# Where late expert weights stand in the DMA queue of an attention-plus-experts kernel

## The chip, the cores and the metric

The kernel runs on one core of a Trainium2 chip. The metric is the device time of one execution in microseconds. Before the change it is 280.02 us (median of 3 runs, 279.81 to 280.1). The profiled execution has a span of 281.0 us. Five engines appear: TensorE (PE, with its weight loads as PEld), VectorE (DVE), ScalarE (ACT), GpSimd (POOL) and SyncE (SP). Data comes and goes through 16 DMA engines.

## What is computed

Windowed attention with a few global positions is followed by a mixture of experts in which each token goes to exactly one expert and each expert takes exactly `cap` tokens, in the order of the gate's scores.

```python
# attention: B, H, S, D = 4, 8, 768, 64; 8 global positions, window of 96
keep = is_global | is_local
scores = np.where(keep, scale * q @ k.T + bias, -1e9)      # bias: slope of the head x distance
x = softmax(scores) @ v                                    # -> (N, D) = (3072, 512)

# experts: E, F = 8, 1024; cap = N // E = 384
for idx in np.argsort(-(x @ w_gate).flatten()):            # greedy, balanced
    tok, e = idx // E, idx % E
    if assigned[tok] < 0 and counts[e] < cap: assigned[tok] = e; counts[e] += 1
for e in range(E):
    mask = assigned == e
    out[mask] = np.maximum(x[mask] @ w1[e], 0.0) @ w2[e]
```

## The kernel before

The kernel has three stages. In the first (to about 145 us) attention is computed, and its result, cast to bf16, is written to a DRAM tensor `x_tok` by DMAs of SyncE. In the second (to about 183 us) the assignment is found by a few rounds on PE and DVE; between these rounds TensorE computes "early work": 128 tokens for each of the experts 0 to 3, whose assignment is certain before the rounds are done. In the third the other tokens go through the eight experts. Each expert has three slabs of 128 tokens; for experts 0 to 3 (`EX = 4`) one slab was early work and two are left.

All weights are fp32 in DRAM and are cast to bf16 by the DMA that loads them. Those of experts 0 and 1 (`W_EARLY = 2`) and 2 come during attention. Those of 3 to 7 are the "late weights": two loads for each expert, in this order, taken from a list one at a time.

```python
def late_tiles(pool, es):
    for e in es:
        w_late[e] = (pool.tile([128, NKC, F_DIM], BF16, ...), pool.tile([128, NFC, DM], BF16, ...))
        lates.append((w_late[e][0], moe_w1[e]...))
        lates.append((w_late[e][1], moe_w2[e]...))
...
late_tiles(w2pool, range(3, N_EXP - 2))          # experts 3, 4, 5
gp = ...tile_pool(name="gp", bufs=9, ...)        # gathered rows, xe
fp = ...tile_pool(name="fp", bufs=2, ...)        # their transposes, xT
hp = ...tile_pool(name="hp", bufs=2, ...)        # hidden layer, hT
op = ...tile_pool(name="op", bufs=4, ...)        # output rows, ot

def late_weights(pin=True):
    if lates:
        dst, s_ = lates.pop(0)
        ins = nc.gpsimd.dma_start(dst, s_)
        if pin:
            tc.keep_in_program_order(ins)

for _ in range(6):                               # at the end of attention
    late_weights(False)
```

Weight loads, gathers of token rows and scatters of output rows are all issued by GpSimd. A gather reads 128 rows of `x_tok` by an index tile; a scatter writes 128 rows of `out` by one.

```python
def gather(e, slabs, pin=True):
    for t in slabs:
        s = TSLAB * e + t
        xe = gp.tile([128, DM], BF16, tag="xe", name=f"xe_{s}")
        ins = nc.gpsimd.indirect_dma_start(out=xe, ..., in_=x_tok[:, :],
                  in_offset=bass.IndirectOffsetOnAxis(ap=idi[:, s : s + 1], axis=0))
        ...
def scatter(ot, ids):
    s = nc.gpsimd.indirect_dma_start(out=out[:, :], out_offset=..., in_=ot, in_offset=None)
    ...
# second stage, when the assignment is known:
dispatch()                                       # writes the index tile idi
for e in range(EX):
    gather(e, range(1, TSLAB), False)            # two slabs for each of experts 0 to 3
```

The tiles of experts 6 and 7 lie in space that attention used, and are made known when the second stage has ended. Then comes the loop of the experts:

```python
late_tiles(w3pool, range(N_EXP - 2, N_EXP))      # experts 6, 7
...
load_x(0)                                        # PE transposes xe, DVE copies to xT
for e in range(N_EXP):
    xT_e = xT_of.pop(e)
    ns = len(slabs(e))
    if first:
        late_weights()
    if e + 2 < N_EXP and not (first and e + 2 < EX):
        gather(e + 2, slabs(e + 2))
    if first:
        late_weights()
    hT = hp.tile([128, NFC, CAP], BF16, tag="hT")
    for fc in range(NFC):                        # first layer: ph, then hT on ACT
        ...
    if e + 1 < N_EXP:
        load_x(e + 1)
    for j, t in enumerate(slabs(e)):             # second layer: po, then ot on DVE
        ...
        scatter(ot, idi[:, TSLAB * e + t : TSLAB * e + t + 1])
```

So in the kernel before the loads of experts 3, 4 and 5 are issued at the end of attention, those of expert 6 in the first round of this loop, those of expert 7 in the second, and the rows of expert 4 in the third.

Of the kernel before, what the change touches and what calls it, by code (L numbers as in the profile page):

```python
# [21 lines left out]
N_EXP = 8  # L22
# [18 lines left out]
EX = 4  # L41
# [4 lines left out]
def kernel(  # L46
# [850 lines left out]
# [4 lines that stand above are left out]
            if pin:  # L901
                tc.keep_in_program_order(ins)

    for _ in range(6):
        late_weights(False)

    def w1_of(e):
# [11 lines left out]
# [4 lines that stand above are left out]
            ins = nc.gpsimd.indirect_dma_start(  # L923
                out=xe, out_offset=None, in_=x_tok[:, :],
# [3 lines that stand above are left out]
            xes[s] = xe  # L928
# [64 lines left out]
    def routing(general):  # L993
      with ExitStack() as dctx:
# [11 lines left out]
        def tok_end():  # L1006
            if held:
                tok_out(*held.pop(0))
# [7 lines left out]
        def bc_e(t):  # L1016
            return t.rearrange("p (c o) -> p c o", o=1).to_broadcast([128, NCHUNK, N_EXP])
# [7 lines left out]
        def work(us):  # L1025
            while us > 0.0 and not general:
                if items:
                    cost, go = items.pop(0)
                    go()
                else:  # L1030
                    cost = 0.22
                    pw = ps_d.tile([128, 512], FP32, tag="po", name="pw")
                    nc.tensor.matmul(pw, lhsT=ident_bf, rhs=w1_early[:, 0, 0, 0:512], start=True, stop=True)
                us -= cost
# [6 lines left out]
        def best(X, Dg):  # L1041
            if X is None:
                UB = Lb
            else:
                nc.tensor.matmul(X, lhsT=negones, rhs=bc_c(Dg), start=False, stop=True)
                UB = Ub
                tok_begin()
                nc.vector.scalar_tensor_tensor(out=Ub[:, 8:32, :].rearrange("p c e -> p (c e)"), in0=X, scalar=0.0,
                                               in1=L_sb.rearrange("p c e -> p (c e)"),
                                               op0=ALU.is_gt, op1=ALU.add)  # L1050
            nc.vector.tensor_reduce(out=mn, in_=UB[:, 8:32, :], axis=AX.X, op=ALU.min)
            return UB
# [230 lines left out]
        if True:  # L1283
            work(0.7)
            X, Dg = None, None
            for kk in ROUND_KS:
                X, Dg = fast_round(kk, X, Dg)
            best(X, Dg)
            work(1.1)
            mnf = rpool.tile([128, NCHUNK], FP32, tag="mnf", name="mnf")  # L1290
            nc.vector.tensor_tensor(out=mnf, in0=mn, in1=cflag, op=ALU.subtract)
            nc.vector.tensor_tensor(out=M, in0=Ub[:, 8:32, :], in1=bc_e(mnf), op=ALU.is_le)
            dispatch()
            for e in range(EX):
                gather(e, range(1, TSLAB), False)
            vt = rpool.tile([128, EC, EX], BF16, tag="vt", name="vt")
            for lo_, hi_, at in ((16, 32, 0), (8, 10, 16)):
                n_ = hi_ - lo_
                nc.vector.tensor_tensor(
                    out=vt[:, at : at + n_, :], in0=Ub[:, lo_:hi_, 0:EX], op=ALU.is_gt,  # L1300
                    in1=mn[:, lo_ - 8 : hi_ - 8].rearrange("p (c o) -> p c o", o=1).to_broadcast([128, n_, EX]))
            nc.vector.tensor_tensor(out=vt, in0=vt, in1=Ck, op=ALU.mult)
            work(1.0)
            pf = ps_d.tile([128, 512], FP32, tag="pk", name="pf")
            nc.tensor.matmul(pf[0:1, 0:CE], lhsT=ones_bf[:, 0:1], rhs=Mf, start=True, stop=True, skip_group_check=True)
            nc.tensor.matmul(pf[0:1, CE : CE + EX * EC], lhsT=ones_bf[:, 0:1], rhs=vt.rearrange("p c e -> p (c e)"),
                             start=True, stop=True, skip_group_check=True)
            fc8 = dap.tile([1, N_EXP + 1], FP32)
            nc.vector.tensor_reduce(out=fc8[:, 0:N_EXP], in_=pf[0:1, 0:CE].rearrange("p (c e) -> p e c", e=N_EXP),
                                    axis=AX.X, op=ALU.add)  # L1310
            nc.vector.tensor_tensor(out=fc8[:, 0:N_EXP], in0=fc8[:, 0:N_EXP], in1=capv, op=ALU.subtract)
            nc.vector.tensor_tensor(out=fc8[:, 0:N_EXP], in0=fc8[:, 0:N_EXP], in1=fc8[:, 0:N_EXP], op=ALU.mult)
            nc.vector.tensor_reduce(out=fc8[:, N_EXP : N_EXP + 1], in_=pf[0:1, CE : CE + EX * EC], axis=AX.X, op=ALU.add)
            fm = dap.tile([1, 1], FP32)
            nc.vector.tensor_reduce(out=fm, in_=fc8, axis=AX.X, op=ALU.max)
            nc.vector.tensor_single_scalar(out=fi, in_=fm, scalar=0.0, op=ALU.is_gt)
            while items:
                work(0.1)
            while deferred:
                tok_begin()  # L1320
                tok_end()

    def experts(first):
        with ExitStack() as fctx:
            ps_t = fctx.enter_context(tc.tile_pool(name="ps_t", bufs=2, space=bass.MemoryType.PSUM))
            ps_h = fctx.enter_context(tc.tile_pool(name="ps_h", bufs=3, space=bass.MemoryType.PSUM))
            ps_o = fctx.enter_context(tc.tile_pool(name="ps_o", bufs=3, space=bass.MemoryType.PSUM))
            xT_of = {}

            def slabs(e):  # L1330
                return range(1 if first and e < EX else 0, TSLAB)

            def load_x(e):
                xT_e = fp.tile([128, NKC, TSLAB, 128], BF16, tag="xT_e", name=f"xT_{e}")
                for j, t in enumerate(slabs(e)):
                    xe = xes.pop(TSLAB * e + t)
                    pxe = ps_t.tile([128, NKC, 128], BF16, tag="pxe")
                    for kc in range(NKC):
                        nc.tensor.transpose(pxe[:, kc, :], xe[:, 128 * kc : 128 * kc + 128], ident_bf)  # L1339
                    nc.vector.tensor_copy(out=xT_e[:, :, j, :], in_=pxe)  # L1340
                xT_of[e] = xT_e

            if not first:
                gather(0, slabs(0))
            load_x(0)
            if not first:
                gather(1, slabs(1))
            for e in range(N_EXP):
                xT_e = xT_of.pop(e)
                ns = len(slabs(e))  # L1350
                if first:
                    late_weights()
                if e + 2 < N_EXP and not (first and e + 2 < EX):
                    gather(e + 2, slabs(e + 2))
                if first:
                    late_weights()
                hT = hp.tile([128, NFC, CAP], BF16, tag="hT")
                for fc in range(NFC):
                    ph = ps_h.tile([128, CAP], FP32, tag="ph")
                    for kc in range(NKC):  # L1360
                        nc.tensor.matmul(ph[:, 0 : 128 * ns], lhsT=w1_of(e)[:, kc, 128 * fc : 128 * fc + 128],  # L1361
                                         rhs=xT_e[:, kc, 0:ns, :].rearrange("p t n -> p (t n)"),
                                         start=(kc == 0), stop=(kc == NKC - 1))
                    nc.scalar.activation(hT[:, fc, 0 : 128 * ns], ph[:, 0 : 128 * ns], AF.Relu)  # L1364
                if e + 1 < N_EXP:
                    load_x(e + 1)
                for j, t in enumerate(slabs(e)):
                    po = ps_o.tile([128, DM], FP32, tag="po")
                    for fc in range(NFC):
                        nc.tensor.matmul(po, lhsT=hT[:, fc, 128 * j : 128 * j + 128],  # L1370
                                         rhs=w2_of(e)[:, fc, :], start=(fc == 0), stop=(fc == NFC - 1))
                    ot = op.tile([128, DM], FP32, tag="ot")
                    nc.vector.tensor_copy(out=ot, in_=po)  # L1373
                    scatter(ot, idi[:, TSLAB * e + t : TSLAB * e + t + 1])
# [53 lines left out]
```

The softmax here doesn't subtract the row's maximum and nothing guards it: scores larger than these inputs give would overflow.

## Time and profile before

| | before |
|---|---|
| time | 280.02 us (279.81 to 280.1) |
| span of the profiled execution | 281.0 us |
| PE busy | 249.5 us, 89% |
| DVE, ACT, POOL busy | 164.0, 142.1, 87.2 us |
| queue 0 (GpSimd's DMAs) | 26.22 MB |
| queue 1 (SyncE's DMAs) | 22.50 MB |
| late weights, as they land | 10 loads of 1024 KB |
| stretch from the first matmul of expert 0 to the last of expert 7 | 186.61 to 271.9 us |

The profile names an operation by its line, its engine and its tiles: `xe<-x_tok,idi` is a gather, `out_dram<-ot,idi` a scatter, `w<-in_moe_w_dram` a late weight load, `pxe<-ident_bf,xe` a transpose of gathered rows, `ph<-xT,w` a matmul of the first layer and `po<-w,hT` one of the second. In a timeline each line has the start and the length in microseconds, and in brackets how long the engine was idle before it and what ended that. A line on POOL for a DMA is the time in which GpSimd issues it, not the transfer.

### The profile page before, as it was taken

What the parts mean: (1) busy time and instruction counts of PE and PEld (TensorE: products, weight loads), DVE (VectorE), ACT (ScalarE), POOL (GpSimd) and SP (SyncE); (2) the same over time, 40 slices, a digit from 0 to 9 for tenths busy, and PEclk for the clock granted to TensorE, in tenths of its full rate; (3) what the DMA queues carried; (4) which work ended last, traced back from release to release, by engine and by line L of the source; (5) the groups of instructions that cost most, each with busy time, mean ns of one, the idle gap of its engine ahead of it and who ended that gap; (6) DMA issues with size and microseconds to landing.
All of it is one profiled execution on the core that took longest, in us unless ns stands there. A gap on an engine that the chain in (4) does not pass through costs nothing. (4 is left out here: it accounts for less than half of the span.)

```text
span 281.0 us, 7775 instructions
## 1 busy us (share of the span) xinstructions
PE 249.5 (89%) x3299; PEld 180.1 (64%) x3299; DVE 164.0 (58%) x346; ACT 142.1 (51%) x240; POOL 87.2 (31%) x145
## 2 busy tenths in 40 slices
PE   7799899999999999999988799867997499999960
PEld 2667687888888888868756666544775255655520
DVE  3978998988879796889257778311222113232120
ACT  5998879595977959534132213222444032523500
POOL 5040000110805720410480001376563444641240
PEclk9999999999999999999999999979999689999995
DMA  7993989499795999499979999735999622320221
GB/s 272 329 251 67 256 183 279 68 235 217 205 268 117 268 179 187 85 189 217 201 138 197 196 216 212 181 106 142 190 243 211 253 85 79 130 93 37 114 79 42
DMA packets 52570, 49.29 MB, mean 175 GB/s; under 512 B 29745, under 2 KB 44081, under 8 KB 52529
## 3 DMA queue, kind: packets, MB, share of 16 engines
q0 software_dynamic: 15680, 26.22, 44.7%
q1 hardware_dynamic: 36848, 22.50, 31.9%
q8 instruction: 28, 0.46, 0.7%
q14 instruction: 14, 0.11, 0.1%
HBM read 56.05 MB, written 9.44 MB: 233 GB/s over the span
## 5 line engine op out<-in xcount | busy, mean ns | idle before, releaser
L1364 ACT ACTIVATE hT<-ph 128x256 bf16<-128x256 f32 (+1 forms) x64 | 27.9, 438 | 55.6 <-PE ph L1361 46.6
L400 ACT ACTIVATE P<-ps 128x860 f32<-128x860 f32 (+1 forms) x46 | 39.4, 896 | 23.2 <-PE ps L382 22.4
L382 PE MATMUL ps<-qT,kA 32*128 32x215 f32 (+2 forms) x864 | 43.4, 333 | 2.5 <-ACT qT L347 2.5
L435 PE MATMUL po<-P,v 128*64 128x215 f32 (+6 forms) x576 | 42.9, 294 | 1.4 <-issue 1.0
L382 PEld LDWEIGHTS ps<-qT,kA 32*128 32x128 f32 x864 | 37.0, 185 | 7.4 <-issue 3.1
L435 PEld LDWEIGHTS po<-P,v 128*64 128x64 f32 x576 | 34.2, 136 | 10.8 <-issue 5.3
L415 DVE TENSOR_TENSOR P<-P,Wm 128x860 f32<-128x860 f32 (+1 forms) x32 | 32.9, 1044 | 6.6 <-ACT P L400 3.9
L1340 DVE COPY xT<-pxe 128x512 bf16<-128x512 bf16 x20 | 8.1, 423 | 46.6 <-PE pxe L1339 38.6
L931 POOL DMA_INDIRECT out_dram<-ot,idi x20 | 19.8, 991 | 37.8 <-DVE ot L1373 36.1
L1373 DVE COPY ot<-po 128x512 f32<-128x512 f32 x20 | 13.8, 692 | 24.8 <-PE po L1370 24.8
L322 DVE STREAM_TRANSPOSE RT<-RT 128x768 f32<-128x768 f32 x28 | 26.2, 959 | 3.5 <-DMA RT<-in_k_dram 3.4
L1370 PE MATMUL po<-w,hT 128*128 128x512 bf16 x112 | 27.7, 401 | 0.0
L466 PE MATMUL pr<-P,onesx 128*32 128x192 f32 (+11 forms) x768 | 27.6, 259 | 0.0
L1370 PEld LDWEIGHTS <-hT 128*128 128x128 bf16 x160 | 15.6, 101 | 18.5 <-issue 2.2
L466 PEld LDWEIGHTS pr<-P,onesx 128*32 128x32 f32 x768 | 24.7, 109 | 2.3 <-issue 0.3
L1361 PE MATMUL ph<-xT,w 128*128 128x384 bf16 (+1 forms) x160 | 25.1, 315 | 0.0
L332 ACT COPY kA<-RT 128x720 f32<-128x720 f32 (+2 forms) x18 | 24.4, 1354 | 0.1
L923 POOL DMA_INDIRECT xe<-x_tok,idi x20 | 19.3, 964 | 14.0 <-issue 4.7
L440 ACT COPY oT<-po 128x384 f32<-128x384 f32 x32 | 14.8, 493 | 13.7 <-PE po L435 7.3
L1361 PEld LDWEIGHTS <-w 128*128 128x128 bf16 x160 | 15.7, 98 | 9.3
L408 DVE TENSOR_TENSOR P<-P,Wm 128x860 f32<-128x860 f32 x16 | 16.5, 1060 | 7.1 <-ACT P L400 7.1
L511 PE MATMUL pk<-ident,oT 128*128 128x128 f32 x96 | 16.5, 287 | 2.1 <-DVE LT L482 2.0
(230 smaller groups left out, 319.2 us busy)
## 6 DMA issues: line engine op xcount, KB each, us to landing
w<-in_moe_w_dram POOLq DMA_DIRECT2D x10, 1024.0 KB
v<-in_v_dram SPq DMA_DIRECT2D x32, 180.0 KB, 3.6
RT<-in_k_dram SPq DMA_DIRECT2D x7, 768.0 KB, 4.5
RT<-in_q_dram SPq DMA_DIRECT2D x7, 768.0 KB, 7.2
w_early<-in_moe_w_dram POOLq DMA_DIRECT2D x8, 512.0 KB
x_tok<-x SPq DMA_DIRECT2D x32, 96.0 KB, 5.1
RT<-in_moe_w_dram POOLq DMA_DIRECT2D x2, 1024.0 KB
w_early<-in_k_dram SPq DMA_DIRECT2D x1, 768.0 KB
```

The costliest lines, as they stand in the source:

```text
L322: nc.vector.transpose(out=t, in_=src[:, :, 32 * g : 32 * g + 32])
L332: nc.scalar.copy(out=kA[:, i0:i1, 8:128].rearrange("p i (c j) -> p i c j", j=NJ), in_=t[:, i0 * NC5 : i1 * NC5, :].rearrange("p (i c) j -> ...
L382: nc.tensor.matmul(heads[a][:, o : o + w], lhsT=kA[r, gd, i, :], rhs=qTt[r, gd, KT * i : KT * i + w], start=(gd == 0), stop=(gd == 1), ski ...
L400: nc.scalar.activation(P[:, :, 0 : GW[g]], ps[w_][:, :, 0 : GW[g]], AF.Exp, scale=0.125)
L415: tt(out=P[:, :, 0 : GW[g]], in0=P[:, :, 0 : GW[g]], in1=Wm[:, h0 : h0 + 2, lo : lo + GW[g]], op=ALU.mult)
L435: nc.tensor.matmul(po[n][bk][64 * t : 64 * t + 64, a - QB * bk : z - QB * bk], lhsT=v7[:, t, i, :], rhs=P[:, t, o + a - q0 : o + z - q0], ...
L466: nc.tensor.matmul(o_, lhsT=l_, rhs=r_, start=first[gq], stop=True, skip_group_check=True)
L923: ins = nc.gpsimd.indirect_dma_start(out=xe, out_offset=None, in_=x_tok[:, :], in_offset=bass.IndirectOffsetOnAxis(ap=idi[:, s : s + 1], a ...
L931: s = nc.gpsimd.indirect_dma_start(out=out[:, :], out_offset=bass.IndirectOffsetOnAxis(ap=ids, axis=0), in_=ot, in_offset=None)
L1361: nc.tensor.matmul(ph[:, 0 : 128 * ns], lhsT=w1_of(e)[:, kc, 128 * fc : 128 * fc + 128], rhs=xT_e[:, kc, 0:ns, :].rearrange("p t n -> p (t ...
L1364: nc.scalar.activation(hT[:, fc, 0 : 128 * ns], ph[:, 0 : 128 * ns], AF.Relu)
L1370: nc.tensor.matmul(po, lhsT=hT[:, fc, 128 * j : 128 * j + 128], rhs=w2_of(e)[:, fc, :], start=(fc == 0), stop=(fc == NFC - 1))
```

## The change

Four loads instead of six are issued at the end of attention (experts 3 and 4). The two of expert 5 are issued behind the first gathers. In the loop, the rows of an expert are gathered three experts ahead instead of two, ahead of that round's weights; the two loads of expert 6 are issued in the third round and those of expert 7 in the fourth. The change is for this: the first gathers and the rows of the fifth expert should find less weight traffic in front of them.

```diff
@@ -901,7 +901,7 @@
-    for _ in range(6):
+    for _ in range(4):
         late_weights(False)
@@ -1293,6 +1293,8 @@
             dispatch()
             for e in range(EX):
                 gather(e, range(1, TSLAB), False)
+            for _ in range(2):
+                late_weights(False)
@@ -1348,11 +1350,11 @@
             for e in range(N_EXP):
                 xT_e = xT_of.pop(e)
                 ns = len(slabs(e))
-                if first:
+                ahead = 3 if first else 2
+                if e + ahead < N_EXP and not (first and e + ahead < EX):
+                    gather(e + ahead, slabs(e + ahead))
+                if first and e in (2, 3):
                     late_weights()
-                if e + 2 < N_EXP and not (first and e + 2 < EX):
-                    gather(e + 2, slabs(e + 2))
-                if first:
                     late_weights()
```

(The hunks are shown without their unchanged edges. `first` is false only in the fallback for assignments that the rounds don't settle; it doesn't run here.)

## The prediction, made before the changed kernel ran

> **What bounds the kernel now.** The chain that ended last breaks off after its last two pieces, so it says nothing about the middle of the run. I read instead, in this order: the table of waits from 150 us on, the TensorE timeline of the eight experts, the GpSimd timeline beside it, and the same stretches as a table with clock and DMA share. TensorE is busy 89% of the span, so its gaps are what can be won. The waits that involve the gathered rows (columns: total us, times, longest):
> ```profile
> PEld L1339 <- DMA xe<-x_tok,idi: 8.5, 4, 5.6
> PE pxe L1339 <- DMA xe<-x_tok,idi: 6.9, 3, 5.3
> POOL xe L923 <- DMA x_tok<-x: 4.0, 1, 4.0
> ```
> PE and PEld are the same wait seen twice. TensorE waits for gathered rows three times, 6.9 us, of which one wait is 5.3. The TensorE timeline (start, length, engine, line, operation, idle before) says where:
> ```profile
> 183.80 0.38 PE L1339 MATMUL pxe<-ident_bf,xe 128*128 128x128 bf16 x4 [0.67 <-ACT otE L978]
> 184.88 0.40 PE L1339 MATMUL pxe<-ident_bf,xe 128*128 128x128 bf16 x4 [0.70 <-DMA xe<-x_tok,idi]
> 186.21 0.61 PE L1339 MATMUL pxe<-ident_bf,xe 128*128 128x128 bf16 x4 [0.92 <-DMA xe<-x_tok,idi]
> ...
> 205.07 3.66 PE L1361 MATMUL ph<-xT,RT 128*128 128x256 bf16 x32
> ...
> 212.46 3.66 PE L1361 MATMUL ph<-xT,w 128*128 128x256 bf16 x32
> 221.39 1.03 PE L1339 MATMUL pxe<-ident_bf,xe 128*128 128x128 bf16 x8 [5.28 <-DMA xe<-x_tok,idi]
> ...
> 223.50 4.81 PE L1370 MATMUL po<-w,hT 128*128 128x512 bf16 x14
> 228.15 5.36 PE L1361 MATMUL ph<-xT,w 128*128 128x384 bf16 x32
> ```
> Expert 2 starts at 205.07, expert 3 at 212.46, expert 4 at 228.15: the third expert took 7.39 us from start to start, the fourth 15.69. Its transposes of expert 4's rows sat 5.28 us behind the gather. Then 14 matmuls took 4.81 us, where expert 2 needs 3.62 for 16. The table by stretch (busy us of PE, PEld, DVE, ACT, POOL; then clock, DMA share, GB/s) gives the reason for that second loss:
> ```profile
> 216.10:221.40 5.30, 0.03 (x2) 0.01 (x1) 0.00 (x0) 0.38 (x1) 0.99 (x1) 0.86 1.08 331
> 221.40:228.20 6.80, 6.80 (x29) 3.35 (x30) 1.97 (x4) 0.00 (x0) 2.86 (x3) 0.60 0.22 69
> 228.20:239.20 11.00, 11.00 (x69) 6.10 (x68) 3.26 (x6) 3.93 (x8) 5.49 (x7) 1.00 0.31 107
> ```
> The granted clock is 0.60 in the stretch after the idle one and 1.00 again later. In the idle stretch the DMA engines are full (share 1.08). The GpSimd timeline says with what:
> ```profile
> 180.82 0.99 POOL L923 DMA_INDIRECT xe<-x_tok,idi  x1 [4.01 <-DMA x_tok<-x]
> ...
> 193.19 1.79 POOL L900 DMA_DIRECT2D w<-in_moe_w_dram  x2
> ...
> 199.87 1.76 POOL L900 DMA_DIRECT2D w<-in_moe_w_dram  x2
> ...
> 207.57 1.00 POOL L923 DMA_INDIRECT xe<-x_tok,idi  x1 [0.30 <-issue]
> ```
> The weights of expert 6 and of expert 7 (four loads of 1024 KB) are issued at 193.19 and 199.87, the rows of expert 4 only at 207.57 and later. They queue behind the weights.
>
> **What the Trainium skill says.** (1) "DMA: Bandwidth & Descriptors", section "Queues, rings and completion order": each engine consumes a ring's descriptors in order, and goes round-robin between queues packet by packet. The trace agrees: rows behind weights on the same queue wait for them, while SyncE's token writes share with them (8.9 us to landing in the stretch 166 to 176, against a median of 5.1). (2) The same page, "Anatomy of one DMA — SWDGE (gpsimd) path": some 2 us fixed per DMA. Here the second gather was issued at 182.12 and TensorE used its rows at 184.88, 2.8 us, of which 1 us is GpSimd's own. (3) "TensorE: Matmul & The Clock Gate", Part 1: half clock after an idle window of about 3.4 us, full clock after a busy one. The trace has clock 0.50 second by second from 186 to 189 and from 220 to 226, after stretches of sparse or no matmuls.
>
> **The change part by part.** The order of instructions is the same on PE, ACT, DVE and SP; only GpSimd's differs. No work is added or removed.
>
> *(a) Expert 4's rows (8.1 us).* They are now gathered in the second expert, ahead of the weights of 6 and 7, with only expert 5's weights ahead of them. Weights move at about 205 GB/s of destination bytes (1.90 MB in the 9 us from 208 to 217, 211 GB/s, all queue 0), so an expert's two loads take 2.1 / 0.205 = 10.2 us. Estimate: gathers 177.5 to 187.6 (eight at 1.27 us), the loads of expert 5 issued until 189.4 and landed about 199; scatters of the early work behind them; expert 4's rows issued about 198 to 202, landed about 204. TensorE wants them after expert 3's first layer, about 214. So the wait goes, and with it the half clock. Expert 3 then costs what expert 2 costs, 7.39, plus 0.22 for a third slab's four transposes: 15.69 - 7.61 = 8.1 us.
>
> *(b) The first gathers (1.4 us).* In the kernel before, six loads from 141.7 keep queue 0 full until about 178; the last four token writes, issued by 171.5, share with them and the first gather waits for them until 180.8. With four loads, queue 0 has 4.2 + 0.5 MB to move after 140; it moved 3.55 MB by 160, so it is empty near 166. The token writes then have the engines for themselves and, at the median 5.1 us, land near 176.5. The gather's other input, the index tile, is written by DVE at 177.15 + 0.18. So the first gather goes at about 177.5, 3.3 us earlier. TensorE cannot use all of it: until 183.80 it has the early experts' second layers, and its new PSUM tiles wait for ACT's last eviction. What goes are the waits of 0.70 and 0.92. The start of expert 0 is then set by two DVE copies (0.42 each) after 183.80: first matmul about 185.2 instead of 186.61, 1.4 us.
>
> *(c) Later weights.* Expert 6: behind expert 5's rows, issued about 210, landed about 221, needed about 241. Expert 7: issued about 219, landed about 234, needed about 252. Rows of 5, 6, 7 are all ahead of their use by over 8 us. Nothing gained, nothing lost.
>
> Sum: 280.0 - 8.1 - 1.4 = **270.5 us**.
>
> **Rivals.**
> *A new wait on output buffers.* There are four `ot` tiles, and expert 3's scatters now stand behind the weights of expert 7 (landed about 234 to 236). Expert 4's third `ot` needs one of those tiles at about 229.5: DVE may stand for 5 us. For it: the queue is in order. Against: three PSUM tiles for `po`, and TensorE needs DVE next only at about 235. Likely cost 0 to 1 us, at worst 4: 271 to 274.5. The same chain in expert 1 (behind expert 5's weights) comes out at about 201 against a need at 202.
> *The bound moves back into expert 0.* In the kernel before, ACT stood 1.75 us twice and DVE 1.7 us once between 190.4 and 195.1, though TensorE had finished their inputs and the DMA engines were half idle. I don't know why. GpSimd was issuing scatters and weight loads then. Expert 0 takes 13.9 us from 183.80, expert 1 takes 7.4. Now expert 5's loads stand in this stretch: this may grow by 2 us (272.5) or vanish (268).
> *The clock of expert 0.* The dip from 186 to 189.4 costs about 1.7 us. TensorE's busy time in the 3.4 us before it rises from about 1.9 to 2.3 us; if that suffices for the full clock, 268.8. I give it one chance in three.
> *The transfer was hidden anyway.* Then the time stays at 280. Against it is the 5.28 us wait itself, named by the trace, with nothing else pending: the second layer of expert 3 was ready on ACT at 216.5.
> *The token writes are not sped up by fewer weights.* Then (b) is lost: 272.
>
> **Range and chances.** The large term stands on one measured wait and 10 us of slack in the new order; I hold it nearly certain. The small ones swing by -2 and +4. Range **267.5 to 274.5**. Over 2% faster means under 274.4: **0.88**; within 2%: **0.10**; slower: **0.02**.
>
> **What would show it right or wrong.** Right: TensorE's 5.28 us wait for `xe` is gone, expert 3 takes about 7.6 us from start to start, no clock of 0.5 after it; the first gather starts near 177.5 with DVE's index tile as its releaser; expert 0 starts near 185.2; from expert 4's start to the end some 53 us as before (281.0 - 228.15). Wrong: a first gather still waiting for `x_tok`; DVE waiting for an `out_dram` landing before `ot` with TensorE standing for it; expert 0 longer than 13 us; a weight wait before expert 5, 6 or 7.

## The result, and the profile after

The changed kernel takes 277.25 us (median of 4 runs, 276.2 to 278.58), the kernel before in the same comparison 280.06. The ratio is 0.990, with a 95% interval of 0.985 to 0.9945: faster by about 1%, not by the 3.4% that was predicted, and outside the predicted range.

The profiled execution has a span of 274.4 us against 281.0. The two profiles are not alike in this: the one before is of an execution of 282.86 us, above all the timed ones (279.81 to 280.87), the one after of the fastest of its four (276.2). So the spans differ by 6.6 us where the medians differ by 2.8. The TensorE timeline of the changed kernel answers to the one shown for the kernel before (start, length, engine, line, operation, idle before):

```profile
181.29 0.61 PE L1341 MATMUL pxe<-ident_bf,xe 128*128 128x128 bf16 x8 [0.67 <-ACT otE L978]
182.26 0.39 PE L1341 MATMUL pxe<-ident_bf,xe 128*128 128x128 bf16 x4 [0.36 <-DVE xT L1342]
182.59 3.65 PE L1363 MATMUL ph<-xT,w_early 128*128 128x256 bf16 x32
...
204.54 3.66 PE L1363 MATMUL ph<-xT,w 128*128 128x256 bf16 x32
208.03 0.61 PE L1341 MATMUL pxe<-ident_bf,xe 128*128 128x128 bf16 x8
...
212.18 5.36 PE L1363 MATMUL ph<-xT,w 128*128 128x384 bf16 x32
...
223.25 5.36 PE L1363 MATMUL ph<-xT,w 128*128 128x384 bf16 x32
228.45 0.61 PE L1341 MATMUL pxe<-ident_bf,xe 128*128 128x128 bf16 x8
228.90 0.60 PE L1372 MATMUL po<-w,hT 128*128 128x512 bf16 x2
237.23 0.59 PE L1341 MATMUL pxe<-ident_bf,xe 128*128 128x128 bf16 x4 [7.73 <-DMA out_dram<-ot,idi]
237.61 6.57 PE L1372 MATMUL po<-w,hT 128*128 128x512 bf16 x22
244.01 5.36 PE L1363 MATMUL ph<-xT,w 128*128 128x384 bf16 x32
```

What the change was made for has happened. No transpose waits for gathered rows any more, and expert 3 takes 212.18 - 204.54 = 7.64 us from start to start where it took 15.69. But two experts later there is a stop that the kernel before did not have: 7.73 us, released by the landing of a scatter, and then 22 matmuls in 6.57 us where expert 4 takes 4.91. Expert 5 takes 244.01 - 223.25 = 20.76 us; expert 4 before it took 11.07.

The DVE timeline of the changed kernel shows who passed the wait on:

```profile
223.77 1.34 DVE L1375 COPY ot<-po 128x512 f32<-128x512 f32 x2 [4.64 <-DMA out_dram<-ot,idi]
236.15 0.69 DVE L1375 COPY ot<-po 128x512 f32<-128x512 f32 x1 [11.04 <-DMA out_dram<-ot,idi]
236.76 0.74 DVE L1342 COPY xT<-pxe 128x512 bf16<-128x512 bf16 x2
237.85 0.42 DVE L1342 COPY xT<-pxe 128x512 bf16<-128x512 bf16 x1 [0.35 <-PE pxe L1341]
```

DVE stood for 11.04 us before it could write expert 4's third output tile (`ot`): there are four, and the one it needed was still being read by a scatter. The copies of expert 6's rows (`xT`) come behind it in DVE's program, and started at 236.76. Their transposes have two PSUM tiles in this kernel, and the third had to wait for the first copy. The GpSimd timeline has the reason why that scatter was late:

```profile
216.37 0.85 POOL L900 DMA_DIRECT2D w<-in_moe_w_dram  x1
218.69 0.93 POOL L900 DMA_DIRECT2D w<-in_moe_w_dram  x1 [1.46 <-issue]
223.82 1.04 POOL L931 DMA_INDIRECT out_dram<-ot,idi  x1 [4.21 <-DMA out_dram<-ot,idi]
```

Both loads of expert 7 are ahead of expert 3's first scatter (223.82) in the same queue. It landed 12.2 us after its issue, just before 236.15; the median of these scatters is 2.8 us. The Trainium skill ("DMA: Bandwidth & Descriptors", "Queues, rings and completion order") states that a DMA engine takes the descriptors of a ring in order; it says so of the rings of SyncE and ScalarE, and this trace agrees for GpSimd's queue. Here it is met from its other side: not rows behind weights but results. The stretches of the changed kernel (busy us of PE, PEld, DVE, ACT, POOL; clock, DMA share, GB/s) complete the picture: full DMA engines, then a reduced clock (0.72), as before in expert 3:

```profile
229.50:237.20 7.70, 0.00 (x0) 0.00 (x0) 1.05 (x3) 0.00 (x0) 2.57 (x4) 0.80 1.17 290
237.20:244.00 6.80, 6.77 (x26) 2.93 (x26) 2.11 (x4) 0.00 (x0) 2.40 (x3) 0.72 0.27 105
```

### The profile page after: what moved, and what is told of

It reads as the page before. It is cut to its first block, busy times and chain, and to the rows that moved or that the text cites. A ratio compares the mean times of both kernels' runs of the same rounds, so it can differ in the third digit from the quotient of the medians.

```text
span 274.4 us, 7770 instructions
## 1 busy us (share of the span) xinstructions
PE 245.6 (90%) x3299; PEld 179.0 (65%) x3299; DVE 163.4 (60%) x346; ACT 142.1 (52%) x240; POOL 87.6 (32%) x145
## 5 line engine op out<-in xcount | busy, mean ns | idle before, releaser
L435 PE MATMUL po<-P,v 128*64 128x215 f32 (+6 forms) x576 | 41.5, 293 | 0.3 <-DVE P L415 0.3
```

The costliest lines, as they stand in the source:

```text
L435: nc.tensor.matmul(po[n][bk][64 * t : 64 * t + 64, a - QB * bk : z - QB * bk], lhsT=v7[:, t, i, :], rhs=P[:, t, o + a - q0 : o + z - q0], ...
```

## The experiments

Each time is a median, with the ratio to the kernel before on the same chip. Runs e1 to e4 were on one chip, e5 to e8 on a second, e9 to e12 on a third; the kernel before takes 280.17, 282.38 and 283.02 us on them. An expert's time is from the first matmul of its first layer to that of the next expert.

**e1: seven output tiles.**

```diff
-op = ...tile_pool(name="op", bufs=4, ...)
+op = ...tile_pool(name="op", bufs=7, ...)
```

Expected: 

> The changed kernel with seven output tiles (ot) instead of four; the order of instructions on every engine is the same. Theory A (the new 7.7 us stop of TensorE in expert 5 comes from DVE standing for an output tile whose scatter is queued behind the weights of expert 7): the stop and the half clock after it (1.7 us) go, about 267.5 to 269 us. Theory B (the queue of GpSimd's transfers is itself the bound, so that the stop only moves to the weights or rows of expert 6 or 7): 274 us or more, with a wait for w or xe. Theory C (the gain was never stable, the times of the changed kernel scatter for another reason): no change from 277.

Measured: 266.55 us (266.5 to 266.62), ratio 0.951 (0.947 to 0.955). Theory A, and a little better than it expected. This is the cleanest of the experiments, because the queue is the same: expert 7's loads are issued at nearly the same time, and the scatters behind them land at the same time. Here are the loads and the scatter in this kernel's GpSimd timeline, and then, in its DVE timeline, the one wait for a landing that is left:

```profile
216.06 0.85 POOL L900 DMA_DIRECT2D w<-in_moe_w_dram  x1
217.61 0.93 POOL L900 DMA_DIRECT2D w<-in_moe_w_dram  x1 [0.71 <-issue]
223.18 1.04 POOL L931 DMA_INDIRECT out_dram<-ot,idi  x1 [4.64 <-DMA out_dram<-ot,idi]
```
```profile
232.85 0.69 DVE L1375 COPY ot<-po 128x512 f32<-128x512 f32 x1 [1.04 <-PE po L1372]
236.29 0.69 DVE L1375 COPY ot<-po 128x512 f32<-128x512 f32 x1 [2.74 <-DMA out_dram<-ot,idi]
240.00 1.32 DVE L1342 COPY xT<-pxe 128x512 bf16<-128x512 bf16 x3 [3.02 <-PE pxe L1341]
```

GpSimd itself stands before this scatter for an earlier landing, 4.64 us here and 4.21 with four tiles, so that wait does not come from the tiles. The landing at about 236.2 has not moved. It now holds the last output tile of expert 5 instead of the last of expert 4, for 2.74 us, and is over before TensorE's next transposes. So it was not the queue's speed that cost some 10 us (9.7 by the two profiled executions, 276.2 and 266.52; 10.7 by the medians), but who had to wait for it.

**e2: four tiles, but the loads behind the scatters** (experts 2 and 3).

```diff
-                if first and e in (2, 3):
-                    late_weights()
-                    late_weights()
                 hT = hp.tile(...)
...
                     scatter(ot, ...)
+                if first and e in (2, 3):
+                    late_weights()
+                    late_weights()
```

Expected: 

> The changed kernel with four output tiles, but in experts 2 and 3 the two weight loads are issued behind that expert's scatters instead of ahead of them. Theory A: expert 3's scatters no longer stand behind the weights of expert 7, so the stop goes although the tiles are still four: 267.5 to 270 us. Theory B: the weights of 6 and 7 land 3 to 5 us later and TensorE stops for them: 275 us or more.

Measured: 267.29 us (266.83 to 268.05), ratio 0.953 (0.949 to 0.957). The stop can also be taken away by the order in the queue. What remains is small: expert 6 takes 12.76 us instead of 11.07, because now the scatters of expert 4 are behind expert 7's weights. DVE still stands for scatters, 4.77 us for expert 4's third tile and 8.66 for expert 5's second, but TensorE's next need of DVE is so near the end of these waits that TensorE stands for 1.77 us only:

```profile
242.19 0.38 PE L1341 MATMUL pxe<-ident_bf,xe 128*128 128x128 bf16 x4 [1.77 <-DVE xT L1342]
```

No wait for weights appeared.

**e3: six loads at the end of attention, the rest of the change as it is.**

Expected: 

> The changed kernel, but with six loads at the end of attention as before (expert 5's two loads go back; the rest of the change stays). It tells what moving expert 5's loads is worth. Theory A: the first gathers wait for the token writes again and cost about 1.4 us at the start of expert 0, but expert 1's output tiles no longer wait behind expert 5's loads, so the loads of 6 and 7 are issued 4 to 6 us earlier and the stop in expert 5 shrinks to 0 to 3 us: 269 to 272.5 us, faster than the changed kernel. If moving expert 5's loads were what makes the gain: 278 us or more.

Measured: 272.98 us (271.39 to 274.56), ratio 0.972 (0.967 to 0.977); a little above the expected 269 to 272.5. The first gathers wait for the token writes again (expert 0 starts 184.44 instead of 182.65 as in e1, and takes 8.82 us instead of 7.16, at reduced clock), and the stop in expert 5 is there with 3.16 us (expert 5: 15.64). It is faster than the changed kernel: by the two profiles, the changed kernel is 3.5 us ahead of it at expert 1's start (1.8 + 1.7) and loses 5.1 us against it in expert 5 (20.76 - 15.64). The expectation had another reason for the shorter stop: the loads of 6 and 7 are issued not 4 to 6 us earlier but 1.5 to 2.2 (206.61, 214.91 and 216.51 against 208.08, 216.37 and 218.69), and the landing that ends the stop comes only 1.3 us earlier (DVE goes on at 234.87 against 236.15). The larger part is that TensorE comes 3.5 us later. What moving expert 5's loads is worth without the stop was not tried.

**e4: the kernel before with seven output tiles.**

Expected: 

> The kernel before with seven output tiles, as a control. Theory A: in the kernel before no wait of TensorE went back to an output tile; only the gathers of expert 5 waited for a scatter's landing. So within 0.5% of 280. If output tiles are a bound of both kernels alike: 272 or less.

Measured: 280.39 us (279.03 to 281.31), ratio 0.9995 (0.997 to 1.002). Four tiles are no bound of the kernel before. They become one through the change.

**e5: the changed kernel with five tiles.**

Expected: 

> The changed kernel with five output tiles, one more than it has. With five, expert 4's third output row tile falls on a tile whose scatter is one of expert 2's, ahead of the weights of expert 7, and expert 1's first no longer waits for a scatter behind expert 5's weights. Theory A: one tile is enough, 266.3 to 268 us, the same as with seven. If it is the number of transfers under way that matters, and not which scatter stands behind which weights: halfway, 270 to 275 us.

Measured: 274.13 us (273.51 to 274.89), ratio 0.969 (0.963 to 0.976), in the range of the rival. But its profile has no wait of DVE for a scatter; the time is lost elsewhere, ahead of expert 1 (see e9).

**e6: rows gathered three experts ahead, nothing else** (on the kernel before).

```diff
-                if first:
-                    late_weights()
-                if e + 2 < N_EXP and not (first and e + 2 < EX):
-                    gather(e + 2, slabs(e + 2))
+                ahead = 3 if first else 2
+                if e + ahead < N_EXP and not (first and e + ahead < EX):
+                    gather(e + ahead, slabs(e + ahead))
                 if first:
                     late_weights()
+                    late_weights()
```

Expected: 

> The kernel before with one part of the change alone: rows gathered three experts ahead, ahead of that round's weights. Six loads at the end of attention, expert 6's weights in the first and expert 7's in the second round, four output tiles, all as before. Theory A: the rows of expert 4 then stand behind one expert's weights only and land about 204, before the need; the scatters behind expert 7's weights are expert 1's, and their tiles are needed about when they land. What is lost against the best version is the wait of the first gathers: 267.5 to 270.5 us, faster than the whole change. If the later weights are what removes the wait: 276 us or more.

Measured: 281.36 us (279.64 to 284.87), ratio 0.996 (0.9935 to 0.999). A miss of theory A by over 10 us. Yet the wait that it spoke of is gone: in the whole profile TensorE waits for gathered rows 1.2 us, both times at the start of expert 0. So the time alone, 276 us or more, does not make the later weights the cause: the rows ahead are enough to remove this wait. The time is in expert 0 (11.14 us), expert 3 (9.90) and expert 4 (13.82), where the kernel of e1 takes 7.16, 7.64 and 11.07; see e11.

**e7: the later weights, with rows two experts ahead.**

Expected: 

> The changed kernel with rows gathered two experts ahead: the other part of the change alone. Theory A: the rows of expert 4 find the queue nearly empty and land just in time, but those of expert 5 now stand behind expert 6's weights and land about 222 against a need of about 217, so a wait for xe of some 5 us comes back, and the output tiles wait as in the changed kernel: 275 to 280 us. If the later weights are enough by themselves: 277 or less with no wait for xe.

Measured: 279.55 us (278.1 to 280.14), ratio 0.988 (0.981 to 0.995). As expected, a wait for rows is back, now for expert 5's, with 3.37 us where some 5 were expected:

```profile
226.99 1.04 PE L1341 MATMUL pxe<-ident_bf,xe 128*128 128x128 bf16 x8 [3.37 <-DMA xe<-x_tok,idi]
```

**e8: the kernel before once more, for its profile.**

Expected: 

> The kernel before once more, for its profile alone. Theory A: whatever time is lost or saved ahead of expert 3's end is taken up by the wait for expert 4's rows, because these land when the queue has worked off the weights, about 219 to 221. If expert 0 starts 2 us earlier than in the first profile and runs at full clock, as in the kernel with seven tiles, the wait is about 9 us instead of 5.3, and the time is the same within 1%.

Measured: 283.96 us, a single execution. Expert 0 was not faster this time (11.24 us), so the case that the expectation speaks of did not arise; the wait is 6.05. It arose in e4, which has the same order of transfers as the kernel before. From the TensorE timelines, the transposes of expert 4's rows in e4, then in e8:

```profile
219.99 1.03 PE L1339 MATMUL pxe<-ident_bf,xe 128*128 128x128 bf16 x8 [8.94 <-DMA xe<-x_tok,idi]
```
```profile
222.71 1.03 PE L1339 MATMUL pxe<-ident_bf,xe 128*128 128x128 bf16 x8 [6.05 <-DMA xe<-x_tok,idi]
```

In e4 expert 0 takes 7.17 us instead of 11.06 in the first profile, and the wait is 8.94 instead of 5.28. Counted from the first transpose of the second stage (143.45 in e4, 144.84 in the first profile, 145.88 in e8) the rows are there after 76.5, 76.6 and 76.8 us. The wait's end is set by the queue. Whatever TensorE loses or wins between is taken up by the wait.

**e9 to e12: four of these once more, together on one chip.**

Expected, e9: 

> The changed kernel with seven output tiles once more, beside the same three kernels on one chip. The profiles so far fall into two kinds: in some, ACT and DVE answer 1.4 to 1.8 us late while GpSimd issues a row of indirect transfers (2.5 us lost near 140, up to 5 in expert 0), in others not. Theory A: without such delays 266.5 us again; with them up to 274, since this kernel has no wait left that could take them up, and then five tiles measure the same as seven.

Expected, e10: 

> The changed kernel with five output tiles once more. Theory A: the 274.1 of the first look came from those delays (7.9 us of them in its profile) and not from the number of tiles; within 1 us of the kernel with seven tiles on the same chip, and no wait of DVE for a scatter in expert 4. If a tile count of five is short: slower than seven by over 2 us with DVE waits for out_dram.

Expected, e11: 

> The kernel before with rows gathered three experts ahead, nothing else, once more. Its first profile had no wait for expert 4's rows, but some 12 us of late answers by ACT and DVE. Theory A: without these 267.5 to 270.5 us, faster than the whole change; with them 278 to 284 as in the first look. If the first look was its true time: 279 or more also where the kernel with seven tiles takes 266.5.

Expected, e12: 

> The changed kernel once more on the same chip. Theory A: its stop in expert 5 ends when the scatters behind expert 7's weights have landed, so delays ahead of it are mostly taken up: 276 to 280 us in either case, and the stop is shorter where expert 0 is longer.

| | time, us | ratio (95%) | second stage starts | expert 0 | expert 3 | expert 4 | expert 5 |
|---|---|---|---|---|---|---|---|
| e1, seven tiles, first chip | 266.55 | 0.951 (0.947 to 0.955) | 142.40 | 7.16 | 7.64 | 11.07 | 11.07 |
| e9, seven tiles | 273.3 | 0.968 (0.962 to 0.973) | 144.58 | 9.84 | 8.02 | 11.07 | 12.78 |
| e10, five tiles | 274.94 | 0.971 (0.965 to 0.977) | 145.88 | 11.69 | 7.72 | 11.07 | 11.43 |
| e11, rows ahead only | 281.4 | 0.995 (0.992 to 0.9975) | 145.78 | 11.09 | 10.14 | 13.95 | 11.07 |
| e12, the changed kernel | 278.24 | 0.985 (0.978 to 0.992) | 144.95 | 9.85 | 8.85 | 11.07 | 16.11 |
| the changed kernel, first profile | 277.25 | 0.990 (0.985 to 0.9945) | 142.31 | 7.16 | 7.64 | 11.07 | 20.76 |

The same kernel with seven tiles takes 266.5 us on one chip and 273.3 on another. The difference of the two profiled executions (273.42 - 266.52 = 6.9) is the sum of four stages of the table: 2.2 + 2.7 + 0.4 + 1.7 = 7.0. In all of them the wait is of one kind, which I call a late answer: ACT or DVE starts late on what TensorE has finished. Ahead of the second stage DVE's transposition starts at 141.62 where it is 138.09 in e1; in expert 5 DVE's first copy of rows starts 2.1 us after the transposes begin, where it is 0.4 in e1. In e9's expert 0 (TensorE, ACT and GpSimd lines of its timeline):

```profile
184.84 1.47 PE L1363 MATMUL ph<-xT,w_early 128*128 128x256 bf16 x12
...
186.46 0.39 ACT L1366 ACTIVATE hT<-ph 128x256 bf16<-128x256 f32 x1 [2.97 <-PE ph L1363]
186.66 0.95 POOL L923 DMA_INDIRECT xe<-x_tok,idi  x1 [0.30 <-issue]
186.89 0.60 PE L1363 MATMUL ph<-xT,w_early 128*128 128x256 bf16 x4 [0.59 <-issue]
187.62 1.80 POOL L900 DMA_DIRECT2D w<-in_moe_w_dram  x2
187.83 0.39 ACT L1366 ACTIVATE hT<-ph 128x256 bf16<-128x256 f32 x1 [0.99 <-PE ph L1363]
```

ACT's first activation needs the first 4 of the 12 matmuls that began at 184.84. In e1 it starts 0.7 us after expert 0's first matmul (183.33 against 182.65); here 1.6 us after it. TensorE then stands for PSUM tiles that ACT has not emptied. Meanwhile GpSimd issues gathers, loads and scatters with pauses of 0.3 us. With this, e10's result can be read: five tiles and seven differ by 1.6 us on that chip, more than the 1 us expected (the two intervals overlap), but e10's profile has no wait of DVE for a scatter in expert 4, and it is longer than e9's in the second stage's start (1.3) and in expert 0 (1.9). It also answers e12: the second stage starts 2.6 us later, expert 0 takes 2.7 us more, and the stop in expert 5 is shorter by 4.7.

e11 stays a miss in part. Its times agree with the expectation "with late answers"; the 268 to 269 us without them is only an estimate (281.2 of the profiled execution less 3.3, 3.9, 2.5 and 2.9 us that its stages have over those of e1 and e3). The estimate takes for granted that no wait takes up a part of the gain, so it is a lower bound of the time. No execution of it without late answers was seen, and the expectation's test by a chip on which seven tiles take 266.5 us was not met either: they take 273.3 here.

## Why the prediction was wrong, step by step

**Step (a), expert 4's rows, 8.1 us: right.** Expert 3 went from 15.69 to 7.64, 8.05 us, and the reduced clock behind it went too.

**Step (b), the first gathers, 1.4 us: right.** From the last early expert's second layer to expert 0's first matmul it was 186.61 - 181.24 = 5.37 us and is 182.59 - 178.73 = 3.86: 1.5 us. The first gather starts 0.8 us after the index tile was written (174.64 + 0.18), and no longer waits for `x_tok`, though the profile names another releaser than DVE:

```profile
175.59 0.98 POOL L923 DMA_INDIRECT xe<-x_tok,idi  x1 [1.31 <-PE pf L1308]
```

In e3, with six loads at the end of attention, it waits for `x_tok` until 178.89, and the same stretch takes 5.58 us.

**Step (c), "nothing gained, nothing lost": wrong for what stands behind the weights.** The weights themselves came in time, as it said. The scatters behind them did not.

**The rival "a new wait on output buffers", "likely cost 0 to 1 us, at worst 4": this is the step that failed.** The chain was the right one, even the tile (expert 4's third) and the landing ("about 234 to 236"; it was 236.0). The same chain in expert 1 came as drawn too: DVE stood 6.60 us, until 201.03, and TensorE did not. But in expert 5 the cost was 9.7 us in the profile: 20.76 - 11.07. The prediction let it cost next to nothing because "TensorE needs DVE next only at about 235"; it did at 229.5. Two things were wrong in that.

First, the schedule was drawn from one profile that had lost 2.5 us before the second stage by late answers and 3.9 in expert 0 by late answers and a reduced clock; in the profile after, these are absent and TensorE came earlier, while the landing did not. DVE's transposition ahead of the second stage, in the kernel before and then in the changed one:

```profile
142.47 0.38 DVE L482 STREAM_TRANSPOSE LT<-pr 128x192 f32<-128x192 f32 x1 [5.96 <-remote]
```
```profile
138.01 0.38 DVE L482 STREAM_TRANSPOSE LT<-pr 128x192 f32<-128x192 f32 x1 [1.65 <-PE pr L469]
```

Second, the loads were drawn too fast. The prediction has an expert's two loads landed some 11 us after their issue ("issued about 210, landed about 221"). In the profile after, the second load of expert 5 landed 14.0 us after its own issue at 186.16, that of expert 6 14.1 us after 208.90; each pair was begun 0.8 us before that, so it took 14.9 us from its first issue. So the stop is there even where TensorE is as late as drawn. In e12 expert 5 starts at 229.75, the loads of 6 and 7 are issued at 210.82, 219.12 and 221.27 (drawn: about 210 and 219), and the tile comes free only at 238.1, for a stop of 5.0 us:

```profile
238.13 0.69 DVE L1375 COPY ot<-po 128x512 f32<-128x512 f32 x1 [9.22 <-DMA out_dram<-ot,idi]
```

The slack that the prediction saw, a need at about 235 against a landing at 234 to 236, was smaller than the errors of its own drawing. Such a slack should be charged with the full loss.

**The rivals of expert 0.** It takes 7.16 us in the profile after, against 11.06. A part of this is the clock, and that rival came true: in the first 3.5 us of expert 0 the granted clock is 1.00 in all eight profiles with four loads at the end of attention, and 0.51 to 0.62 in five of the six with six loads (e4 is the exception, with 1.00). e3 against e1 measures it where there are no late answers: 8.82 - 7.16 = 1.7 us, the size that the prediction gave it. The rest of the 3.9 us, some 2.2 by difference, was luck: with late answers the changed kernel takes 9.85 us there too (e12). (The clock of 0.50 that the prediction reads "second by second" is read microsecond by microsecond.)

The sum for the two first profiles: 2.5 (late answers, ahead of the change) + 1.5 + 3.9 + 8.05 - 9.7 = 6.3, of 6.6 by the spans; the 2.5 and some 2.2 of the 3.9 are not the change's. For the medians, e1 says it best: without the stop the change is worth 280.17 - 266.55 = 13.6 us on that chip, and the stop gives some 10 back. On the third chip it is 283.02 - 273.3 = 9.7 us, of which the stop gives 4.9 back (e12 against e9). The 9.5 us predicted was too small for the first chip and blind to the stop: the wait for rows in the kernel before was worth more than the 5.28 us of its profile, as late answers ahead of it had used up a part.

The fastest version is the changed kernel with seven output tiles: 0.951 on one chip, 0.968 on another.

## What to carry to other kernels

When bulk loads are moved back in a queue, list every small transfer behind them and ask which buffer its landing frees, and which engine needs that buffer next; an output tile is as good a stop as an input. One wait hides the losses ahead of it: with its end set by a queue, its length in one profile is neither the gain of removing it nor a constant. A spare tile can cut such a chain: one more was enough for the wait in expert 4 to go (e5, e10), and three more cost the kernel before no time (e4).

## What was not expected of the hardware

In the runs on two of the three chips, and in the first profile of the kernel before, ACT and DVE answer finished TensorE work late while GpSimd issues a row of DMAs: about 1 us for each answer of ACT in e9's expert 0, 3.5 us for DVE's transposition ahead of its second stage, 7 us in all in its profile of 273.42 us. None is to be seen in e1's profile of the same kernel, whose four times lie within 0.12 us, though GpSimd issues the same row there. What makes the difference between the chips, and whether GpSimd's issuing is the cause at all, was not tried and stays open.
